# An order table for TensorE and VectorE in a fused attention and maxout kernel

## The chip, the cores and the metric

One core of one Trainium2 chip runs the whole kernel. The metric is the device time of one execution in microseconds (us); the median over several executions counts.

## The reference

Attention with queries pooled in pairs, then a feed-forward layer that takes the larger of two projections:

```python
# q, k, v: (8, 8, 1152, 64); w1, w2: (512, 1024); w_out: (1024, 512)
q_pool = q.reshape(B, H, S // 2, 2, D).mean(axis=3)
scores = (1.0 / np.sqrt(D)) * np.matmul(q_pool, k.transpose(0, 1, 3, 2))
attn = np.exp(scores - scores.max(-1)); attn = attn / attn.sum(-1)   # axes kept
x = np.matmul(attn, v)            # to (4608 tokens, 512), heads side by side
g = np.maximum(x @ w1, x @ w2)
out = g @ w_out                   # (4608, 512)
```

## The kernel before

**The work.** The 64 heads are taken two at a time: 32 pairs, four pairs to a batch. For each pair, GpSimd casts q, k and v to bf16 (`cast_q` adds the two pooled rows), k is transposed by a DMA (`ktrans`) or, for the first five pairs, on TensorE (`ktrans_pe`), and q by eight 32-partition transposes on VectorE (`qtrans_dve`, L378) or, for the first five pairs, on TensorE.

The scores of all pairs are one long row of columns, cut into 324 groups of 512 columns. One *score group* (`scores`, L516) is 2 to 8 matmuls; the two heads use rows 0 to 63 and 64 to 127 of the array. Its result fills one of the buffers `sps` (two PSUM banks), and ScalarE takes the exponential of it (L523) into the SBUF ring `et`. At first there are three such buffers. Once feed-forward work begins, at some 60 us, one of them is given to other work and the scores alternate between two (`ring`).

When all groups of a pair are through, its *weighted sums* come (`av_jobs`): one *rest block* with 64 columns of the array (18 matmuls, L437) and eight units of nine matmuls (L425), into two further banks. VectorE divides by the row sums (`norm`, L447 to L457) into `xnat`. A finished batch is transposed into `xT` by five DMAs (`xtrans`, L564); the first and the last batch are transposed on TensorE (`xtrans_pe`).

The feed-forward layer is computed as max(x w1, x w2) w_out = relu(x (w1 - w2)) w_out + x (w2 w_out). `h_pairs` (L728) makes the relu input and `p_pair` (L761) the output, in *units* of two matmuls of 64 rows each, which run beside each other on the two halves of the array; VectorE evacuates two banks at once (L737, L772). The second half of such a job swaps the two halves, and its first unit is a *fence*: it waits until TensorE's last write to these banks is complete. After the last score, the same work goes in single-bank jobs on all 128 rows (L701, L794), with ScalarE helping to evacuate. The weights are prepared in the first third (`w_cast`, `w_diff`, `w2t_job`, `w21_jobs`).

**Order.** Nothing is looped on the chip. The function plays through the work with a clock of its own: at each step it picks the next TensorE operation from the jobs in `lane`, by estimated readiness (`when`), rank and estimated cost (`op(..., cost=...)`). Its model has one cost per operation, a fixed signalling delay per engine (`LAT`), 0.1 us where TensorE's shape (`mode`) changes, and a single DMA pipe. What it emits stands in `plan.ops`, each operation with the operations it depends on (`deps`). `solve` then turns dependences into semaphore waits: it walks the list in order and leaves out every wait that an earlier wait of the engine already implies. `emit` writes each engine's operations in their order in the list, so an engine whose next operation isn't ready stops. Three orders hang together in this way: TensorE's 1471 operations, VectorE's 516, and those of ScalarE (370), GpSimd (105) and the DMA queue on SyncE (210).

The five modes of TensorE operations are "s" (two halves of 64 rows: scores and feed-forward pairs), "f" (all 128 rows: weighted sums, transposes and single-bank jobs), "c" (64 columns: rest blocks), and "z" (64 by 64: transposes of q). In the order before, neighbours differ in mode at 204 places.

Of the kernel before, what the change touches and what calls it, by code (L numbers as in the profile page):

```python
# [1 line left out]

# [9 lines left out]
COPY = mybir.ActivationFunctionType.Copy  # L12
ALU = mybir.AluOpType
AX = mybir.AxisListType


class Plan:
# [40 lines left out]
    def op(self, eng, fn, r=(), w=(), dma=None, cost=0.1, mode="f", after=(), solo=False,  # L58
           fence=False):
        n = len(self.ops)  # L60
        assert all(k in self.writer for k in r), r
        deps, raw = self.deps(r, w, after)
        prev = self.last.get(eng)
        if prev is not None and (solo or self.ops[prev]["solo"]):
            deps.add(prev)
            raw.add(prev)
        self.last[eng] = n
        t = self.when(eng, r, w, after, fence)
        if dma is not None:
            if not self.dma_free:  # L70
                t = 0.78
            self.free[eng] = t + (1.3 if mode == "t" else 0.5)
            a = max(self.free[eng] + 1.2, self.dma_free)
            self.dma_free = a + cost + (1.9 if a < 5.0 <= a + cost else 0.0)
            seen = self.dma_free + 0.7
        else:
            if eng == "PE" and mode != self.mode:
                t += 0.1
                self.mode = mode
            self.free[eng] = t + cost  # L80
            seen = t + cost + self.LAT[eng]
        self.ops.append(dict(eng=eng, fn=fn, deps=deps, raw=raw, dma=dma, w=tuple(w),
                             seen=seen, end=self.free[eng], solo=solo, fence=fence))
        for k in r:
            self.readers.setdefault(k, set()).add(n)
        for k in w:
            self.writer[k] = n
            self.readers[k] = set()
        return n

    def solve(self):
        ops = self.ops
        know = {}
        dma_seen = {}
        for n, o in enumerate(ops):
            eng = o["eng"]
            kn = know.setdefault(eng, {})
            o["waits"] = []
            for d in sorted(o["deps"], reverse=True):
                p = ops[d]  # L100
                if p["dma"] is None:
                    if p["eng"] == eng and not o["fence"] and (eng == "PE" or eng != "DVE" and d not in o["raw"]):
                        continue
                    key = p["eng"]
                else:
                    key = ("dma", p["dma"])
                if kn.get(key, -1) >= d:
                    continue
                o["waits"].append(d)
                for k, v in p["know"].items():  # L110
                    if kn.get(k, -1) < v:
                        kn[k] = v
                kn[key] = max(kn.get(key, -1), d)
            o["know"] = dict(kn)
            if o["dma"] is not None:
                dma_seen[o["dma"]] = dma_seen.get(o["dma"], 0) + 1
                o["count"] = 16 * dma_seen[o["dma"]]
        need = set()
        for o in ops:
            need.update(o["waits"])  # L120
        cnt = {}
        for n, o in enumerate(ops):
            if o["dma"] is None:
                o["inc"] = n in need
                if o["inc"]:
                    cnt[o["eng"]] = cnt.get(o["eng"], 0) + 1
                    o["count"] = cnt[o["eng"]]
        self.dma_total = {k: 16 * v for k, v in dma_seen.items()}
# [33 lines left out]
def bass_funnel_attn__then__act_maxout2_kernel(  # L162
# [32 lines left out]
    with ctx:  # L195
# [41 lines left out]
        plan = Plan()  # L237
# [8 lines left out]
        def setup():  # L246
            op("POOL", lambda g: g.memset(ident[:, :], 1.0), w=["id0"])
            op("POOL", lambda g: g.affine_select(
                ident[:, :], ident[:, :], pattern=[[1, P]], compare_op=ALU.is_equal,
                fill=0.0, base=0, channel_multiplier=-1), r=["id0"], w=["ident"])  # L250

            def ones(g):
                for s in range(3):
                    last = g.memset(vE[s][:, :, :, 64:66], 1.0)
                return last

            op("POOL", ones, w=["vE0", "vE1", "vE2"])
# [76 lines left out]
        def dve(fn, r, w, cost):  # L334
            op("DVE", fn, r=r, w=w, cost=cost)
# [267 lines left out]
        def w_cast(part, ct):  # L603
            if part == 0:
                dve(lambda e: e.tensor_reduce(
                    w2b[:, ct, :], w2f[:, ct, :].unsqueeze(2), AX.X, ALU.max),
                    [f"w2f{ct}"], [f"w2b{ct}"], 1.13)
            else:
                dve(lambda e: e.tensor_reduce(
                    wo[:, 2 * ct:2 * ct + 2, :], wof[:, 2 * ct:2 * ct + 2, :].unsqueeze(3), AX.X, ALU.max),  # L610
                    [f"wof{ct}"], [f"wo{2 * ct}", f"wo{2 * ct + 1}"], 1.13)
# [240 lines left out]
        line = []  # L852
# [5 lines left out]
        todo = []  # L858
# [135 lines left out]
        def burst_size():  # L994

            if turn_at[0] < NGR:
                return 1
            done = [b for b in range(B) if all(av_half.get(b * NHP + j) == 2 for j in range(NHP))]
            return 3 if done else 2
# [188 lines left out]
        while p_end[0] < NTOK:  # L1188
# [48 lines left out]
            else:  # L1237
# [3 lines left out]
                size = burst_size()  # L1241
# [10 lines left out]
        plan.free["PE"] = 1e9  # L1252
        flush()

        plan.solve()
        engines, dmas = plan.sems()
        sem = {n: ctx.enter_context(nc.semaphore("sem_" + n)) for n in engines + dmas}
# [49 lines left out]
```

## Time and profile before

| | |
|---|---|
| median of 7 runs | 378.08 us (377.7 to 380.06) |
| the profiled execution | 378.93 us, of which 377.2 us span |
| TensorE matmul busy | 360.3 us (96%) |
| ScalarE busy | 315.0 us (84%) |
| VectorE busy | 238.0 us (63%) |
| GpSimd busy | 124.9 us (33%) |
| granted TensorE clock | 1.0 throughout |
| last score group starts | 326.4 us |

The span is from the first to the last instruction of the profiled execution. Busy time of TensorE is modelled at the end of each matmul, and a matmul that stands waiting for its weights counts in part as busy; its starts are measured.

### The profile page before, as it was taken

The page shows a single profiled execution, that of the slowest core. Times are in us where ns is not written, and L with a number is a line of the kernel's source. Part 1 is how long each engine was busy: PE and PEld are TensorE (multiplying, and loading weights), DVE is VectorE, ACT ScalarE, POOL GpSimd, SP SyncE. Part 2 cuts the span into 40 slices and gives each one's busy share as a digit, 9 for nine tenths or more (in the row PEclk, how much of TensorE's full clock was granted, in tenths as well). Part 3 has the DMA queues.
Part 4 walks back from the last instruction along what each step waited for, and adds up shares of the span by engine and source line. Part 5 has one row for each costly group of instructions (what it writes and reads, how often), then busy time and mean ns, then how long its engine had stood idle before and what let it go on. Part 6 is the DMA issues. An engine that isn't in the chain of part 4 may idle for free.

```text
span 377.2 us, 12699 instructions
## 1 busy us (share of the span) xinstructions
PE 360.3 (96%) x5621; PEld 203.1 (54%) x5621; DVE 238.0 (63%) x516; ACT 315.0 (84%) x360; POOL 124.9 (33%) x111
## 2 busy tenths in 40 slices
PE   4899999999999999999999999998999999999996
PEld 2465556555555464555555555554655554665463
DVE  2685499866677667765686668765786635342231
ACT  4999799999999999999999999999899999811131
POOL 1359955562234233333333333332233010000000
PEclk9999999999999999999999999999999999999999
DMA  7999999999999799978898979997994431012324
GB/s 291 406 396 400 398 234 321 326 323 328 126 313 324 225 211 235 312 225 232 209 339 236 258 159 339 291 235 85 257 282 112 97 80 34 2 29 59 82 57 111
DMA packets 76823, 84.68 MB, mean 224 GB/s; under 512 B 49376, under 2 KB 49632, under 8 KB 76768
## 3 DMA queue, kind: packets, MB, share of 16 engines
q1 hardware_dynamic: 75888, 82.56, 79.3%
q10 hardware_dynamic: 880, 1.31, 0.9%
q8 instruction: 44, 0.72, 0.9%
q14 instruction: 11, 0.09, 0.1%
HBM read 62.91 MB, written 9.44 MB: 192 GB/s over the span
## 4 chain that ended last, share of the span: by engine, by line
PE 68%; ACT 19%; DVE 9%; issue 2%; DMA 1%; SPq 0%; DVEq 0%
ACT et L523 19%; PE sps L516 15%; PE sps L425 9%; PE sps L761 8%; PE fb L425 7%; PE sps L794 6%; DVE qpT L378 5%; PE fb L761 5%; PE fb L728 4%; PE sps L728 4%; PE sps L701 2%; PE fb L701 2%; PE sps L437 2%; PE fb L794 1%; PE fb L437 1%
## 5 line engine op out<-in xcount | busy, mean ns | idle before, releaser
L523 ACT ACTIVATE et<-sps 128x1024 bf16<-128x1024 f32 (+1 forms) x336 | 304.0, 1033 | 18.4 <-PE sps L516 17.0
L516 PE MATMUL sps<-qpT,kT 64*128 64x256 bf16 (+7 forms) x1162 | 120.4, 290 | 5.1 <-ACT et L523 1.7
L378 DVE STREAM_TRANSPOSE qpT<-qp 32x288 bf16<-32x288 bf16 x216 | 101.4, 469 | 34.1 <-PE sps L516 25.2
L324 POOL TENSOR_SCALAR vE<-vraw 128x1152 bf16<-128x1152 f32 x32 | 36.9, 1153 | 150.0 <-PE sps L425 89.9
L516 PEld LDWEIGHTS sps<-qpT,kT 64*128 64x128 bf16 x1162 | 39.8, 94 | 81.2 <-ACT et L523 64.6
L318 POOL TENSOR_TENSOR qp<-qraw 128x576 bf16<-128x576 f32 x30 | 42.1, 1404 | 12.3 <-DMA qraw<-in_q_dram 6.6
L425 PE MATMUL fb<-vE,et 128*128 128x65 bf16 x1152 | 40.7, 193 | 0.1
L425 PE MATMUL sps<-vE,et 128*128 128x65 bf16 x1152 | 40.4, 193 | 0.0
L425 PEld LDWEIGHTS fb<-vE,et 128*128 128x128 bf16 x1152 | 36.7, 97 | 4.9 <-issue 3.7
L285 POOL TENSOR_SCALAR kbf<-kraw 128x1152 bf16<-128x1152 f32 x31 | 35.7, 1151 | 10.3 <-DMA kraw<-in_k_dram 7.9
L425 PEld LDWEIGHTS sps<-vE,et 128*128 128x128 bf16 x1152 | 36.5, 97 | 4.1 <-issue 3.5
L728 PE MATMUL fb<-xT,wd 64*128 64x512 bf16 (+1 forms) x240 | 35.9, 373 | 1.6 <-issue 1.3
L728 PE MATMUL sps<-xT,wd 64*128 64x512 bf16 x224 | 33.0, 376 | 0.0
L761 PE MATMUL sps<-wo,stage 64*128 64x512 bf16 x224 | 31.9, 376 | 0.0
L761 PE MATMUL fb<-wo,stage 64*128 64x512 bf16 x192 | 27.6, 376 | 0.0
L737 DVE TENSOR_SCALAR stage<-fb 128x1024 bf16<-128x1024 f32 (+1 forms) x15 | 18.1, 1204 | 12.3 <-PE fb L728 12.2
L737 DVE TENSOR_SCALAR stage<-sps 128x1024 bf16<-128x1024 f32 x14 | 17.1, 1220 | 12.3 <-PE sps L728 11.9
L728 PEld LDWEIGHTS fb<-xT,wd 64*128 64x128 bf16 x240 | 11.2, 94 | 11.9 <-PE fb L728 2.1
L761 PE MATMUL sps<-w,xT 64*128 64x512 bf16 x112 | 16.6, 378 | 0.8 <-DVE xnat L457 0.6
L772 DVE COPY stage<-sps 128x1024 f32<-128x1024 f32 x7 | 8.6, 1223 | 12.2 <-PE sps L761 12.2
L794 PE MATMUL sps<-wo,stage 128*128 128x512 bf16 (+2 forms) x72 | 15.8, 355 | 0.0
L761 PEld LDWEIGHTS sps<-wo,stage 64*128 64x128 bf16 x224 | 10.7, 94 | 8.3 <-issue 0.4
(68 smaller groups left out, 278.3 us busy)
## 6 DMA issues: line engine op xcount, KB each, us to landing
kraw<-in_k_dram SPq DMA_DIRECT2D x32, 576.0 KB, 7.1
vraw<-in_v_dram SPq DMA_DIRECT2D x32, 576.0 KB, 7.8
qraw<-in_q_dram SPq DMA_DIRECT2D x31, 576.0 KB, 6.2
out_dram<-stage SPq DMA_DIRECT2D x19, 256.0 KB, 4.8
out_dram<-stage SPq DMA_DIRECT2D x23, 128.0 KB, 2.4
xT<-in_moe_w_dram SPq DMA_DIRECT2D x4, 512.0 KB, 10.1
stage<-in_moe_w_out_dram SPq DMA_DIRECT2D x4, 512.0 KB, 13.6
stage<-in_moe_w_dram SPq DMA_DIRECT2D x4, 512.0 KB, 13.6
```

The source lines that it names most:

```text
L285: op("POOL", lambda g: g.tensor_scalar(kbf[s][:, :, :, :].rearrange("p t h d -> p h t d"), kraw[r][:, :, :, :], 1.0, 1.0, ALU.mult, ALU.mu ...
L318: op("POOL", lambda g: g.tensor_tensor(qpf[s][:, :, :], qraw[r][:, :, 0, :], qraw[r][:, :, 1, :], ALU.add), r=[f"qraw{r}"], w=[f"qp{s}.0", ...
L324: op("POOL", lambda g: g.tensor_scalar(vE[r][:, :, :, 0:D].rearrange("p t h d -> p h t d"), vraw[r][:, :, :, :], 1.0, 1.0, ALU.mult, ALU.m ...
L378: op("DVE", lambda e: e.transpose(view[dst:dst + 32, :, 32 * pb:32 * pb + 32], qpf[s][src:src + 32, :, 32 * db:32 * db + 32]), r=[f"qp{s}. ...
L425: last = e.matmul(fb[m][:, sb * 66:sb * 66 + 65], et[:, a:a + P], vE[vs][:, t, half, 0:65], start=(t == 0), stop=(t == NT - 1))
L516: last = e.matmul(sps[r][:, h, col:col + hi - lo], kT[i % 3][rows(h), t, :], qpT[i % 3][rows(h), lo:hi], start=True, stop=True)
L523: op("ACT", lambda e: e.activation(et2[:, :, c:c + z - a], sps[r][:, :, a - g * W:z - g * W], EXP, scale=scale), r=[f"s{r}"], w=keys + ([f ...
L701: return e.matmul(fb[m][:, 0:size], wd[:, ct, ft * P:(ft + 1) * P], xT[:, ct, n0:n1], start=(ct == 0), stop=(ct == NC_ - 1))
L728: last = e.matmul(fb[m + k][:, 0:size], wd[z, ct, (f0 + k) * P:(f0 + k + 1) * P], xT[z, ct, n0:n1], start=(turn == 0 and ct == 0), stop=(t ...
L737: dve(lambda e: e.tensor_scalar_max(gT[:, f0:f0 + 2, g0:g0 + size], wide[m // 2][:, :, 0:size], 0.0), [f"f{m}", f"f{m + 1}"], w + [f"f{m}" ...
L761: last = e.matmul(fb[m + k][:, :], lhs, rhs, start=(turn == 0 and j == 0), stop=(turn == 1 and j == NC_ + NF - 1))
L794: return e.matmul(fb[m][:, 0:c1 - c0], lhs, rhs[:, c0:c1], start=(j == 0), stop=(j == NC_ + NF - 1))
```

## The change

Two strings are added, one for TensorE and one for VectorE. Each character (with a "~" ahead of it for a distance over 39) says which of the operations that are left, in the order in which the planner emitted them, comes next: "0" the first, "1" the second, and so on. `arrange` takes the planner's list, deals it out by engine, puts the two engines in the order of the strings, and merges the engines' lists again so that each operation stands behind those that it depends on. `solve` then works on the new list. The dependences are those of the order before; the operations themselves, and the order on ScalarE, GpSimd and the DMA queue, are as they were.

```diff
+ORDER = {
+    "PE": (
+        "0000100100020000101000100002003003010021030001000000000201000101100002:0088:09080062220051333533"
...
+    ),
+    "DVE": (
+        "0000000010101000000020010200000000000000010000044857000200122210?0603354544492119265250304134727"
...
+    ),
+}
...
+    def arrange(self, order):
+        line = {}
+        for n, o in enumerate(self.ops):
+            line.setdefault(o["eng"], []).append(n)
+        for eng, picks in order.items():
+            rest = line[eng]
+            line[eng] = [rest.pop(40 * (len(c) - 1) + ord(c[-1]) - 48) for c in re.findall("~*[0-X]", picks)]
+            assert not rest
+        at = {key: 0 for key in line}
+        new = {}
+        ops = []
+        while len(ops) < len(self.ops):
+            size = len(ops)
+            for key, todo in line.items():
+                while at[key] < len(todo) and all(d in new for d in self.ops[todo[at[key]]]["deps"]):
+                    n = todo[at[key]]
+                    at[key] += 1
+                    new[n] = len(ops)
+                    ops.append(self.ops[n])
+            assert len(ops) > size
+        for o in ops:
+            o["deps"] = {new[d] for d in o["deps"]}
+            o["raw"] = {new[d] for d in o["raw"]}
+        self.ops = ops
...
         plan.free["PE"] = 1e9
         flush()
 
+        plan.arrange(ORDER)
         plan.solve()
```

A stretch of TensorE's order before, and about the same stretch after, with S for a score group, h and p for feed-forward units (L728, L761), r for a rest block, a for a weighted-sum unit, and a count where one repeats:

```
before  S r a3 S S a5 S h S h4 S h3 S h3 S h3 S h2 S h3 S r a3 S S a5 S h S p3 S
after   S h2 r S h2 S a4 S S a4 S h3 S h3 S h3 S h3 S h3 S h2 S h3 S h r S a4 S S a4 S h3 S p3 S
```

More of the change, by code (lines that the diff above doesn't have):

```diff
@@ L1 @@
+import re
 from contextlib import ExitStack
@@ L14 @@
 AX = mybir.AxisListType
+ORDER = {
+    "PE": (
+        "0000100100020000101000100002003003010021030001000000000201000101100002:0088:09080062220051333533"
+        "330022004060220100344353340000400005500000001001101107445440024005000511611005006002041000300400"
+        "030004;05026330220040050005000050030005611100500004060000500004000030060003003055000060700006000"
+        "600060006004474450007115007:000:000904:0020900080000800004:9044404830000600700006007222071004:;;"
+        "9::;;908400247011060006000600060000700500;90030590100060070000600777<788787777070000060070400600"
+        "603305200041114104000500300014500005000400003053022420104;<<4;;90:80060004360006007777;887888870"
+        "7000805580448400800006007000777<9086666800744900090004888070005007600799997844445000604063026000"
+        "60005006000702522226722226000600060006000600085:555:75555500070007605700373307010600005007305222"
+        "26722220600061116010600060000500700500080335:0000080:0000900080000700080062692557:52229000900090"
+        "0090009000:05899959:8555:000:006:600:030:0119100080009047444489444490009001911108119110080000900"
+        "005090030059000070007000060060000500702223842225226007111160006000600085:55859755550007000700474"
+        "44700006000040666668666666600040555044504034335000040000300003<304000033000002000200300202100000"
+        "001000010000000000000000010000000004002803355152412210000000000000000000000000000000000000000000"
+        "000000000000000000000000000000000000000000000000000000000000000000000000000000000000000000000000"
+        "000000000000000000000000000000000000000000000000000000000000000000000000000000000000000000000000"
+        "0000000000000000000000000000000"
+    ),
+    "DVE": (
+        "0000000010101000000020010200000000000000010000044857000200122210?0603354544492119265250304134727"
+        "120130277343331538;8777035094853=022331222208818240454486361160005995655340220=550845212=3016472"
+        "0042664334:09;8278714048102577541033333331603577065504453>>:0999421057:244072020421331121;;<0676"
+        "60150455975132444413302:;0;999083>8;23:02988877003033626240022233248;7415;;78772104230==919880?1"
+        "61224920773065534436>44100343333303;;;;2::0082034:8:;:;;2920025<<8<;<<;6231105443122211110000010"
+        "000010000000000000000000000000000000"
+    ),
+}
 class Plan:
```

## The prediction

> **What bounds the kernel now.** I read the page's head first, for which engine is full; then busy time by stage, the totals of waits, and one repeating stretch of the timeline. The first fence is the page (busy time with its share of the span, then 40 slices in tenths).
>
> ```profile
> span 377.2 us, 12699 instructions
> PE 360.3 (96%) x5621; PEld 203.1 (54%) x5621; DVE 238.0 (63%) x516; ACT 315.0 (84%) x360; POOL 124.9 (33%) x111
> ...
> PE   4899999999999999999999999998999999999996
> ...
> ACT  4999799999999999999999999999899999811131
> ```
>
> TensorE is full to the end, ScalarE until 326 us, where the last softmax exponential is done. What follows, 51 us of feed-forward work, has TensorE alone. The view by stage (stretch, length, then busy us of PE, PEld, DVE, ACT, POOL):
>
> ```profile
> 60.00:326.00 266.00, 261.11 (x4372) 144.63 (x4370) 185.39 (x402) 251.91 (x279) 90.19 (x74) 1.00 0.87 226
> ```
>
> So the 266 us in the middle carry 252 us of ScalarE. TensorE's 261 is too flattering, since a matmul counts as busy while its weights wait; its slack has to be found in starts. Waits (engine, tile, line, releaser: us, times, longest):
>
> ```profile
> PEld sps L516 <- ACT et L523: 64.6, 180, 1.0
> ...
> ACT et L523 <- PE sps L516: 17.0, 39, 2.5
> ```
>
> The two engines wait for each other: scores (L516) need a free score buffer, which the exponential (L523) gives back, and the exponential needs scores. The 64.6 us are mostly covered by the matmul in front; the 17.0 us are bare. The timeline shows one turn of the pattern (start, us, engine, line, count, idle before):
>
> ```profile
> 108.86 0.39 PE L516 MATMUL sps<-qpT,kT 64*128 64x320 bf16 x4
> 109.18 0.47 PE L437 MATMUL sps<-vE,et 128*64 128x65 bf16 x18
> 109.59 0.99 PE L425 MATMUL sps<-vE,et 128*128 128x65 bf16 x27
> 110.51 0.61 PE L516 MATMUL sps<-qpT,kT 64*128 64x384 bf16 x8
> 111.06 1.53 PE L425 MATMUL sps<-vE,et 128*128 128x65 bf16 x45
> 112.52 0.39 PE L516 MATMUL sps<-qpT,kT 64*128 64x512 bf16 x2
> 112.75 0.38 PE L728 MATMUL fb<-xT,wd 64*128 64x512 bf16 x2
> 112.96 0.38 PE L516 MATMUL sps<-qpT,kT 64*128 64x512 bf16 x2
> 113.18 0.81 PE L728 MATMUL fb<-xT,wd 64*128 64x512 bf16 x6
> 113.83 0.38 PE L728 MATMUL sps<-xT,wd 64*128 64x512 bf16 x2
> 114.04 0.38 PE L516 MATMUL sps<-qpT,kT 64*128 64x64 bf16 x4
> 114.26 0.81 PE L728 MATMUL sps<-xT,wd 64*128 64x512 bf16 x6
> 114.94 0.39 PE L516 MATMUL sps<-qpT,kT 64*128 64x128 bf16 x4
> ```
> ```profile
> 110.94 7.61 ACT L523 ACTIVATE et<-sps 128x1024 bf16<-128x1024 f32 x8 [0.30 <-PE sps L516]
> ```
>
> Prices from starts. A score group S is 0.22 us (114.04 to 114.26). A feed-forward unit (two matmuls) is 0.216 (113.18 to 113.83 is three). A weighted-sum unit (nine matmuls, L425) is 0.272: 111.06 to 112.52 is five, and 0.10 over. That 0.10 comes at each change of the array's shape: S to a weighted sum takes 0.314 over the trace where S to a feed-forward unit takes 0.218, and the last weighted-sum unit before an S takes 0.367 where one before its like takes 0.272. So **a switch costs 0.095**. In steady state a score comes each 0.917 us: ScalarE's pace.
>
> Taking for each kind of neighbours its usual unhindered distance from each actual distance leaves 24.3 us of TensorE stall: 7.6 before 60 us, 16.1 from 60 to 320, 0.6 later. The ending stretch isn't stalled. In the middle, some 80 scores after a feed-forward unit start 0.04 late and 17 start 0.25 late; there are single losses of 0.47 (three times), 0.69, and this one, where a feed-forward unit came before its input (no engine is named; its source is an xT transpose by DMA):
>
> ```profile
> 263.67 0.82 PE L728 MATMUL fb<-xT,wd 64*128 64x512 bf16 x6 [1.32 <-issue]
> ```
>
> **What the skill says.** The Trainium skill, page "TensorEngine Tiling (Array Packing)", section Key Properties: changing the tiling mode drains TensorE. The trace agrees: 0.095 us at each change between 64-row, 128-row and 64-column matmuls, nothing between two users of one shape. Page "TensorE: Matmul & The Clock Gate", Part 3, The mechanism: a weight load is pulled ahead of running matmuls where it doesn't conflict. That agrees with the scores that waited being 0.04 late at the least: their weights couldn't be ahead. Page "Perfetto Trace Analysis", section Tensor Engine Instruction: a matmul's end is an estimate; hence starts alone are used here.
>
> **The change, part by part.** Read against the kernel's own list, the TensorE table moves 1099 of 1471 operations, by 12 places earlier to 22 later; the VectorE table 437 of 516, by 15 earlier to 24 later. Nothing is added or removed, and ScalarE, GpSimd and the DMA queue keep their order. The last score stays at the same place with the same work ahead of it, and TensorE's list behind its 1206th entry is unchanged. So the end moves as the last score moves; ScalarE and VectorE in the tail only follow.
>
> *Added: switches.* 204 become 240: 36 x 0.095 = **+3.4 us**, 31 of them after 60 us (2.9). Fifteen are column-tiled rest blocks (L437) straight before scores, a pair the trace lacks. Nearest row: rest block to weighted sum, the same sort of switch, 0.407 with the block. Bounds: 0 to 0.2 each, so 0 to 3 us; I take 0.095.
>
> *Removed: stall.* Name a gap by the units between two scores: c the rest block, a4 four weighted sums, 3 three feed-forward units. Before, a turn is mostly "3 3 3 2 3 ca3 0 a5 1 4". With the prices a 3 is 0.218 + 3 x 0.216 = 0.866, under ScalarE's 0.917, so TensorE waits 0.05 each time and 0.27 at the 2; ca3 is 0.321 + 0.407 + 2 x 0.272 + 0.367 = 1.64, which two buffers don't cover: the exponential starts 0.30 us after its engine went idle, some 0.4 off its pace (the ACT line above). TensorE's sum is 9.27 us for ten scores; the 0.46 that it waits and the 0.57 that ScalarE starves (0.4 at ca3, 0.17 at a5) make 9.73.
>
> After, threes drop from 109 to 76 and fours rise from 18 to 44, and the weighted sums are cut oftener: "3 3 3 3 3 1c a4 0 a4" is typical. Sum: 5 x 0.866 + 0.913 + 1.497 + 0.228 + 1.497 = 8.47 for nine, against 9 x 0.917 = 8.25 for ScalarE. Followed by hand from a state in which scores just wait: 1c meets its buffer on time, the first a4 starves ScalarE by 0.26, the 0 waits 0.11, the second a4 starves nobody, and the next threes run 0.01 to 0.27 behind their buffers, so none waits. Stall is 0.11 at most against 0.46, at the price of one or two switches.
>
> Limit of the gain: TensorE needs 266 - 16.4 (stall, 60 to 326) + 2.9 = 252.5 us in the middle, ScalarE its 251.9. Two engines this level, with two buffers between, don't both run full. Of 16.4 us I leave 7: 27 turns at 0.11 (3.0), about 60 scores that still find their weights late (2.4), half of the single losses (1.6). The saving is 16.4 - 7 - 2.9 = **6.5 us**. Before 60 us I take zero: there ScalarE is busy without a break from 20 to 40 us and the loads move 400 GB/s, so half a microsecond of switches stands against as much regained.
>
> *Moved on VectorE.* Evacuations and normalisations go 2 to 5 places earlier, the transposes of q (L378, 0.469 us each) 5 later on the mean. Queued behind a transpose is at worst an evacuation of 1.22 us that frees two banks. I cost this at nothing: VectorE is 63% busy, and a transposed q is wanted most of a turn later. In the new list the nearest reuse of a bank comes 1.41 us of TensorE work after its last writer, as against 0.88 before; the work from the last weighted sum of a batch to the first unit on its transposed rows grows in four places by 0.5 to 2.8 us (by 1.0 where 1.3 was lost) and shrinks in three by 0.23 at most. If that cover is gone, each late evacuation stops TensorE for up to 0.5 us, as three did. Stores issue as evacuations end, so on the SP queue they don't come later.
>
> Sum: the profiled run took 378.93 us (span 377.2), 0.85 above the median of 378.08. 378.93 - 6.5 = 372.4, or on the median's footing **371.6**. Bounds: all stall but the start's gone, 365; switches at their dear end and a stall of 9 left, 375.
>
> **Rivals.** (1) ScalarE becomes the bound: exponentials pause at each fresh split, and TensorE's waits come back as score waits. For it: 252 against 252.5. Half the intended saving is left, about 375. (2) The gain is hidden: VectorE or DMA lateness gives it back at transposed inputs, as at 263 us; 378. Against it: those distances grow. (3) **Slower**: the switches aren't repaid. Place: the cut weighted sums; price: 3.4 us at 0.095, up to 5 with dear rest blocks. It decides once less than 3.4 of the stall goes, so if scores still wait 0.04 and 0.25 as often as before: 382. Against it: the hand-followed turn. (4) The table does nothing: excluded in its letter, as most places move.
>
> **How the numbers follow.** 0.3% (1.1 us) is about what a measurement of this kernel can tell from no change. Forecast (367 to 375) 0.68; rival 1, 0.12; rival 2, 0.06; rival 3, 0.14. Faster 0.80, same 0.06, slower 0.14. The range goes from 366 to 378.6: it leaves out the slow case and a little below.
>
> **What would show it.** Right: the wait of L523 for L516 falls from 17.0 to under 10 us; the last score starts at 320 instead of 326.4; the 1.32 at the block after 260 us shrinks; matmul counts and the last 51 us stay. Wrong: L523's wait unchanged with more L425-to-L516 switches (rival 3), or new VectorE releasers in front of L728 and L761 (rival 2).

## The result and the profile after

The changed kernel takes **380.87 us** in the median (378.36 to 383.75, 24 runs), the kernel before 377.92 (377.4 to 380.86, 61 runs): a recorded ratio of **1.0063**, 95% interval 1.0047 to 1.0079 (it is not the quotient of the medians, which is 1.0078; the later ratios are taken in the same way). It is slower, by less than one per cent, where the prediction said 371.6 and faster. The profiled execution took 382.42 us, 380.3 of it span. It is one of five executions of the change, of 382.4 to 383.8 us, that were granted 0.996 of the clock; the others, of 378.4 to 381.9 us, were granted 0.998 or more.

The head of the changed kernel's page: busy time, then the slices of TensorE, ScalarE and of TensorE's clock.

```profile
span 380.3 us, 12682 instructions
## 1 busy us (share of the span) xinstructions
PE 359.4 (95%) x5621; PEld 212.1 (56%) x5621; DVE 237.0 (62%) x516; ACT 316.4 (83%) x360; POOL 124.5 (33%) x111
...
PE   3799989999999999999978999999999999999996
...
ACT  4999899999999999999968999999989999811131
...
PEclk9999999999999999999989999999999999999999
```

The work is the same. TensorE and ScalarE have a dent at 190 to 209 us, the 21st and 22nd slice, and the clock one in the 21st. By stage, ScalarE did less in the middle 266 us than before (249.7 us against 251.9):

```profile
60.00:326.00 266.00, 258.77 (x4338) 152.01 (x4339) 184.05 (x401) 249.72 (x276) 88.52 (x73) 0.99 0.84 226
```

The waits (line numbers are 56 higher than before: scores L572, exponential L579, normalisation L503 to L513, q transposes L434, feed-forward units L784 and L817):

```profile
PEld sps L572 <- ACT et L579: 24.5, 84, 1.5
ACT et L579 <- PE sps L572: 18.4, 39, 2.5
...
PEld sps L817 <- DVE xnat L513: 4.4, 6, 1.5
...
PEld fb L784 <- DVE xnat L513: 2.8, 5, 0.9
```

TensorE's wait for the exponential fell from 64.6 to 24.5 us, as intended. What is new is feed-forward units that wait for a normalisation. Before, the same two rows had 1.2 us, shown here, and 0.7 us:

```profile
PEld sps L761 <- DVE xnat L457: 1.2, 2, 0.6
```

ScalarE still lacks scores for 18.4 us, so the 40 us bought nothing on its side.

TensorE's stall from 60 to 328 us, by what ended it, in this and all later profiles. It is worked out as in the prediction: start-to-start time less the usual one for the pair of operations, put to the last of the operations waited for. "None" is stall for which none of these ended less than 0.25 us before; parts under 0.5 us in sum are left out, and the parts of a row miss its total by up to 0.7 us. The kernel before comes to 14.1 us here, where the prediction counted 16.1 for 60 to 320 us; only differences between rows are used.

| us | score buffer | normalisation | evacuation, q transposes | DMA | fence | none | all |
|---|---|---|---|---|---|---|---|
| before | 9.5 | 1.6 | 0.6 | 1.5 | 0.9 | 0.0 | 14.1 |
| the change | 2.7 | 5.7 | 1.3 | 0 | 0.8 | 3.7 | 13.7 |
| e1, transposes back | 2.7 | 2.5 | 4.7 | 0 | 0.7 | 4.1 | 14.2 |
| e2, VectorE's table alone | 4.4 | 22.2 | 8.2 | 0 | 1.3 | 6.5 | 43.3 |
| e3, short transposes, change | 3.4 | 1.0 | 0 | 0 | 0.2 | 0.5 | 4.9 |
| e4, short transposes, planner | 10.8 | 0.6 | 0.4 | 0 | 1.6 | 0.1 | 13.6 |
| e5, VectorE relisted | 3.4 | 0.6 | 0 | 0 | 0.4 | 1.3 | 5.3 |
| e8, planner, VectorE relisted | 10.0 | 0.6 | 0.4 | 0.5 | 1.2 | 0.2 | 13.0 |
| e6, light loads, change | 2.9 | 5.5 | 1.3 | 0 | 0.2 | 0.1 | 9.8 |
| e7, light loads, planner | 9.8 | 1.6 | 0.5 | 0 | 0.9 | 0.0 | 12.8 |

The span closes on it: no change of stall before 60 us (11.8 in both), -0.4 in the middle, +3.4 for the 36 switches, which makes 3.0 of the 3.1 us.

So of the score waits 6.8 us went, and the lost DMA wait of 1.5. They came back as 4.1 of normalisations, 0.7 of evacuations and transposes, and 3.7 for which no operation answers. Here is a late normalisation, in the timeline of VectorE and of TensorE (changed kernel):

```profile
270.86 1.22 DVE L793 TENSOR_SCALAR stage<-fb 128x1024 bf16<-128x1024 f32 x1 [2.37 <-PE fb L784]
272.38 1.23 DVE L828 COPY stage<-sps 128x1024 f32<-128x1024 f32 x1 [0.29 <-PE sps L817]
273.63 3.72 DVE L434 STREAM_TRANSPOSE qpT<-qp 32x288 bf16<-32x288 bf16 x8
277.39 0.19 DVE L503 RECIPROCAL rc<-sps 128x5 f32<-128x5 f32 x1
277.62 0.45 DVE L508 TENSOR_TENSOR xnat<-sps,rc 64x64 bf16<-64x64 f32 x2
278.10 0.42 DVE L513 TENSOR_TENSOR xnat<-sps,rc 128x256 bf16<-128x256 f32 x1
278.44 0.17 DVE L503 RECIPROCAL rc<-sps 128x4 f32<-128x4 f32 x1
278.65 0.42 DVE L513 TENSOR_TENSOR xnat<-sps,rc 128x256 bf16<-128x256 f32 x1
```
```profile
276.15 1.26 PE L481 MATMUL sps<-vE,et 128*128 128x65 bf16 x36
277.35 0.39 PE L572 MATMUL sps<-qpT,kT 64*128 64x64 bf16 x4
277.58 0.81 PE L784 MATMUL fb<-xT,wd 64*128 64x512 bf16 x6
278.22 0.38 PE L572 MATMUL sps<-qpT,kT 64*128 64x128 bf16 x4
279.13 1.04 PE L784 MATMUL sps<-xT,wd 64*128 64x512 bf16 x8 [0.52 <-DVE xnat L513]
```

VectorE first stands idle for 2.37 us with an evacuation at its head, whose bank TensorE hasn't written yet. Four of the eight transposes behind it had had their inputs since 259 us. When it may go on, all eight run in a row until 277.35. The bank of the pair's first half has its last sum in the first of the four units that start at 276.15 and is complete at some 276.6, so its normalisation starts 0.8 us late; the second half's bank is complete at 277.4. The two normalisations stand in one block of 1.7 us that ends at 279.07, and TensorE's next unit, which needs these banks, starts 0.69 us late.

The 3.7 us without a releaser are one event, TensorE's timeline at 191 us and the stretches around it (length, busy times, then the clock, DMA share and GB/s):

```profile
190.97 0.81 PE L784 MATMUL fb<-xT,wd 64*128 64x512 bf16 x5
193.73 0.58 PE L784 MATMUL fb<-xT,wd 64*128 64x512 bf16 x1 [1.96 <-issue]
193.74 1.00 PE L572 MATMUL sps<-qpT,kT 64*128 64x512 bf16 x2
```
```profile
194.00:197.00 3.00, 3.00 (x18) 1.64 (x16) 0.00 (x0) 1.54 (x2) 0.41 (x1) 0.50 1.02 387
197.00:200.00 3.00, 3.00 (x38) 1.97 (x36) 1.77 (x3) 2.76 (x4) 0.00 (x0) 0.98 0.96 359
```

One of two matmuls of a unit runs, and its twin starts 2.3 us later (2.1 of it stall), with no semaphore between; then TensorE runs at half clock for 3.4 us (0.50 in the first stretch). The page names a small queue:

```profile
q8 instruction: 44, 0.72, 0.8%
```

I read its 44 pieces of 16 KB as TensorE's own instructions, 256 each: 44 x 256 is 11,264, TensorE has 11,242 matmuls and weight loads, and a piece comes for about every 256 of them. In the trace a piece usually starts to arrive when TensorE is 200 to 400 instructions past the last but one boundary, if the count has a boundary at each 256. Piece 22 of the changed kernel (counted from 0) starts at 191.5 us, at 449. It has landed at 192.4, and TensorE doesn't advance until 193.7. Before, the same piece started at 233 instructions, and the latest of all at 393.

### The profile page after: what moved, and what is told of

Same layout as the page of the kernel before. It is cut to its first block, busy times and chain, and to the rows that moved or that the text cites. A ratio compares the mean times of both kernels' runs of the same rounds, so it can differ in the third digit from the quotient of the medians.

```text
span 380.3 us, 12682 instructions
## 1 busy us (share of the span) xinstructions
PE 359.4 (95%) x5621; PEld 212.1 (56%) x5621; DVE 237.0 (62%) x516; ACT 316.4 (83%) x360; POOL 124.5 (33%) x111
## 4 chain that ended last, share of the span: by engine, by line
PE 67%; DVE 11%; ACT 9%; issue 7%; DMA 3%; POOL 2%; SPq 0%; POOLq 0%; DVEq 0%
PE sps L572 15%; ACT et L579 9%; PE sps L817 8%; PE sps L481 7%; PE fb L481 7%; PE fb L817 6%; PE sps L784 6%; PE sps L850 5%; DVE qpT L434 5%; PE fb L784 4%; DMA qraw<-in_q_dram 2%; PE sps L757 2%; DVE xnat L513 2%; PE fb L757 2%; PE fb L695 1%
## 5 line engine op out<-in xcount | busy, mean ns | idle before, releaser
L579 ACT ACTIVATE et<-sps 128x1024 bf16<-128x1024 f32 (+1 forms) x336 | 305.4, 1015 | 19.9 <-PE sps L572 18.4
L572 PE MATMUL sps<-qpT,kT 64*128 64x256 bf16 (+7 forms) x1162 | 122.3, 290 | 3.8 <-ACT et L579 1.9
L434 DVE STREAM_TRANSPOSE qpT<-qp 32x288 bf16<-32x288 bf16 x216 | 100.1, 467 | 9.7 <-POOL qp L374 2.5
L572 PEld LDWEIGHTS sps<-qpT,kT 64*128 64x128 bf16 x1162 | 46.4, 95 | 60.4 <-ACT et L579 24.5
L481 PE MATMUL sps<-vE,et 128*128 128x65 bf16 x1152 | 41.7, 193 | 0.0
L784 PE MATMUL fb<-xT,wd 64*128 64x512 bf16 (+1 forms) x240 | 38.0, 380 | 2.7 <-issue 2.0
L784 PE MATMUL sps<-xT,wd 64*128 64x512 bf16 x224 | 35.8, 383 | 1.2 <-DVE xnat L513 0.7
L817 PE MATMUL sps<-wo,stage 64*128 64x512 bf16 x224 | 31.7, 376 | 0.0
L817 PE MATMUL fb<-wo,stage 64*128 64x512 bf16 x192 | 28.1, 376 | 0.0
L793 DVE TENSOR_SCALAR stage<-fb 128x1024 bf16<-128x1024 f32 (+1 forms) x15 | 18.0, 1202 | 13.6 <-PE fb L784 13.3
L503 DVE RECIPROCAL rc<-fb 128x5 f32<-128x5 f32 (+1 forms) x32 | 5.9, 185 | 25.8 <-PE fb L481 25.5
L503 DVE RECIPROCAL rc<-sps 128x4 f32<-128x4 f32 (+1 forms) x32 | 5.9, 183 | 23.0 <-PE sps L481 22.7
L817 PE MATMUL sps<-w,xT 64*128 64x512 bf16 x112 | 17.1, 378 | 2.3 <-DVE xnat L513 2.0
L784 PEld LDWEIGHTS fb<-xT,wd 64*128 64x128 bf16 x240 | 11.3, 95 | 10.7 <-DVE xnat L513 2.8
L784 PEld LDWEIGHTS sps<-xT,wd 64*128 64x128 bf16 x224 | 10.3, 95 | 12.0 <-PE sps L784 2.2
## 6 DMA issues: line engine op xcount, KB each, us to landing
stage<-in_moe_w_dram SPq DMA_DIRECT2D x4, 512.0 KB, 14.2
```

The source lines that it names most:

```text
L434: op("DVE", lambda e: e.transpose(view[dst:dst + 32, :, 32 * pb:32 * pb + 32], qpf[s][src:src + 32, :, 32 * db:32 * db + 32]), r=[f"qp{s}. ...
L481: last = e.matmul(fb[m][:, sb * 66:sb * 66 + 65], et[:, a:a + P], vE[vs][:, t, half, 0:65], start=(t == 0), stop=(t == NT - 1))
L572: last = e.matmul(sps[r][:, h, col:col + hi - lo], kT[i % 3][rows(h), t, :], qpT[i % 3][rows(h), lo:hi], start=True, stop=True)
L579: op("ACT", lambda e: e.activation(et2[:, :, c:c + z - a], sps[r][:, :, a - g * W:z - g * W], EXP, scale=scale), r=[f"s{r}"], w=keys + ([f ...
L784: last = e.matmul(fb[m + k][:, 0:size], wd[z, ct, (f0 + k) * P:(f0 + k + 1) * P], xT[z, ct, n0:n1], start=(turn == 0 and ct == 0), stop=(t ...
L793: dve(lambda e: e.tensor_scalar_max(gT[:, f0:f0 + 2, g0:g0 + size], wide[m // 2][:, :, 0:size], 0.0), [f"f{m}", f"f{m + 1}"], w + [f"f{m}" ...
```

## The experiments

**Theory A**: the new TensorE order does save the score waits, and VectorE's order gives them back, because its fixed places put q transposes ahead of normalisations. **Theory B**: the new TensorE order isn't better; late normalisations are a symptom. **Theory C**, for the rest: TensorE's instructions came late among the transfers.

### e1: q transposes back in their old places

```diff
 VectorE's list: (t a transpose, r/x/n a normalisation, E an evacuation)
-the change's list
+its other 300 operations in the change's order; each t again behind as many of them as in the planner's list
```

> TensorE's table as in the change; in VectorE's table only the 216 q transposes (L434 in the changed kernel) are put back to their old places among the other VectorE operations (on the mean 4.7 places earlier), the rest keeps the new order. Theory A (the gain was real and was given back by normalisations that stand behind q transposes): TensorE's waits for normalisations, 5.7 us after 60 us in the changed kernel, fall to about 2, its waits for score buffers stay near 2.7 (9.5 before); the time is 373 to 376. Theory B (the new TensorE order is no better, and the late normalisations are a symptom): score-buffer waits come back as the others go, the time is 378 or more.

Measured: 381.06 us (379.87 to 384.02), ratio 1.0077 (1.0048 to 1.0106). Neither theory's picture came. Normalisation waits fell to 2.5 and score waits stayed at 2.7, as A has it, but 4.0 us of evacuation waits appeared. VectorE and TensorE of this run:

```profile
150.51 1.23 DVE L793 TENSOR_SCALAR stage<-fb 128x1024 bf16<-128x1024 f32 x1 [1.91 <-PE fb L784]
151.65 1.90 DVE L434 STREAM_TRANSPOSE qpT<-qp 32x288 bf16<-32x288 bf16 x4
153.56 1.22 DVE L793 TENSOR_SCALAR stage<-sps 128x1024 bf16<-128x1024 f32 x1
```
```profile
154.84 0.47 PE L493 MATMUL sps<-vE,et 128*64 128x65 bf16 x18 [1.24 <-DVE stage L793]
```

The old places don't suit the new TensorE order: four transposes now stand ahead of an evacuation, and the rest block that needs its bank stops for 1.24 us. The stall without a releaser came at the same operation (2.5 us at 197.9). The time is in B's range and not in A's, but the score waits that B asks for didn't come back. The wait moved; the run doesn't decide between A and B.

### e2: VectorE's table without TensorE's

```diff
 ORDER = {
-    "PE": (...),
     "DVE": (...),
```

> VectorE's table alone, TensorE in the planner's order. Theory A: score waits as before (about 9.5 us), no added switches (204), but normalisations late behind transposes as in the changed kernel, some 2 to 4 us more of them: 380 to 383. Theory B: VectorE's order is no cost of its own: 377.5 to 379.

Measured: 419.23 us (415.92 to 421.27), ratio 1.1065 (1.102 to 1.111), far outside both. TensorE waits 22 us for normalisations. One of them, in TensorE's timeline of this run:

```profile
79.79 0.61 PE L766 MATMUL fb<-xT,wd 64*128 64x512 bf16 x2 [3.33 <-DVE xnat L495]
```

The bank had its last sum at 75.2 us. VectorE worked all the time between, on transposes and on the other half's normalisation, which its list puts ahead. The half clock, for 3.4 to 6.8 us, shows up five times: once at 20 us, and four times behind idle stretches of TensorE of 2.2 to 3.5 us. What the run teaches isn't the price of VectorE's table in the changed kernel, where the two tables fit far better, but how steep the price of a misfit is.

### e3 and e4: short q transposes

```diff
-                view[dst:dst + 32, :, 32 * pb:32 * pb + 32],
-                qpf[s][src:src + 32, :, 32 * db:32 * db + 32]),
+                view[dst:dst + 32, 0:4, 32 * pb:32 * pb + 32],
+                qpf[s][src:src + 32, 0:4, 32 * db:32 * db + 32]),
```

> The changed kernel with both tables, but each q transpose by VectorE moves 4 of its 9 column blocks, so its result is not the reference's; the count and the order of operations and all waits stay. VectorE gets some 45 to 55 us less work. Theory A: the waits for normalisations fall from 5.7 to under 2 us and the time to 374 to 376, well under its control with the planner's order. Theory B: no nearer than before, within 1 us of the control or above it.

> The control of the last one: the planner's order (a table of its own places, so that the merging of the list is in it), q transposes of 4 of 9 blocks. Theory A: 1 to 2 us less than before at the most (normalisations cost TensorE 1.6 us there): 376 to 378. Theory B: the same, and the changed order with short transposes is not below it.

The two kernels leave out five of nine blocks of each q transpose. Measured: 373.92 us with the change's order (372.79 to 375.79; ratio to before 0.9886, 0.9857 to 0.9914), 377.95 with the planner's (377.2 to 380.6; 0.9996, 0.9982 to 1.0011). VectorE's busy time fell by 35 us (237.0 to 202.4; 45 to 55 were expected). The short transposes do nothing for the planner's order and 7 us for the change's: normalisation waits go from 5.7 to 1.0, score waits rise only to 3.4, and piece 22 of the instructions came in time, which is part of the 7 us. That is A against B: the TensorE order is 4 us better than the planner's once VectorE is out of its way. Its last score starts at 320.4 us, where the prediction had 320.

The trace of e4 also holds the instruction stall, in the planner's order. TensorE stops inside one weighted-sum unit at 21.9 us, at 449 instructions past the last but one boundary, while piece 0 arrives (21.4 to 22.4), and 3.4 us at half clock follow from 23.9:

```profile
23.98 0.46 PE L481 MATMUL fb<-vE,et 128*128 128x65 bf16 x5 [1.86 <-issue]
```

A second, shorter stop of this kind at 194.5 us, inside a score group and at 445 instructions, is about 0.6 of the 1.6 us that the table puts to the fence.

### e5 and e8: VectorE listed anew

```diff
 VectorE's list, a stretch of it:
-n t r t x r t t x n n t t t E t t t E E ...
+n n t8 r x x r n n E t3 E E ...
```

TensorE's table stays. For e5, VectorE's operations behind the first q transpose are sorted along the TensorE times of e3: what empties a bank goes first once the bank is written; transposes fill the rest, unless a bank falls due within 0.3 us. For e8 the same rule is used along the times of the kernel before, with the planner's TensorE order.

> TensorE's table as in the change, full q transposes, and a new order for VectorE alone: behind the first q transpose its operations are listed anew along the TensorE times of the run with short transposes, an evacuation or a normalisation ahead of any transpose once its bank is written, a transpose where none of these falls due within 0.3 us. Theory A (the gain of the TensorE order is real, and where VectorE's transposes stand decides whether it is kept): waits for normalisations and evacuations together, 6.4 us after 60 us in the changed kernel and 7.2 with the transposes put back, fall below 2.5; score waits stay near 3; 373 to 376. Theory B (VectorE hasn't the room, whatever the order): 378 to 381, with the same waits in other places.

> The control of the relisted run: TensorE in the planner's order, VectorE listed anew by the same rule along the times of the kernel before. Theory A: normalisations and evacuations cost TensorE 2.2 us after 60 us before, so at most 1 to 2 us come off, and the score waits of 9.5 us stay: 376.5 to 378.5. If the relisting alone made the gain, it would be at 375 too.

Measured: e5 **373.12 us** (371.52 to 373.97), ratio 0.9871 (0.985 to 0.9892); e8 377.76 (377.11 to 380.22), ratio 1.0 (0.9985 to 1.0016). e5 does the full work in the change's TensorE order, and takes 7.7 us less than with the change's VectorE table. Not all of it is waits for VectorE: at piece 22 TensorE stands idle for 0.8 us instead of 2.0, and no half clock follows. e5 beats both kernels, and e8 says that the sorting by itself gains nothing. Here are the head of the page and the waits of e5:

```profile
span 370.4 us, 12692 instructions
## 1 busy us (share of the span) xinstructions
PE 355.5 (96%) x5614; PEld 210.2 (57%) x5621; DVE 239.0 (65%) x516; ACT 314.2 (85%) x360; POOL 125.0 (34%) x111
```
```profile
PEld sps L572 <- ACT et L579: 33.3, 111, 1.5
...
ACT et L579 <- PE sps L572: 11.2, 28, 1.2
...
PEld sps L817 <- DVE xnat L513: 0.5, 1, 0.5
```

VectorE is as busy as ever; only its order differs. Feed-forward units hardly wait for normalisations (0.5 us in the row that had 4.4), and now ScalarE's bare wait for scores is down too, from 17.0 before to 11.2. The same place as in the changed kernel's timeline above:

```profile
263.52 1.23 DVE L828 COPY stage<-sps 128x1024 f32<-128x1024 f32 x1 [0.29 <-PE sps L817]
264.77 2.88 DVE L434 STREAM_TRANSPOSE qpT<-qp 32x288 bf16<-32x288 bf16 x6
267.78 0.20 DVE L503 RECIPROCAL rc<-sps 128x5 f32<-128x5 f32 x1
...
269.05 0.42 DVE L513 TENSOR_TENSOR xnat<-sps,rc 128x256 bf16<-128x256 f32 x1
```
```profile
269.37 0.38 PE L572 MATMUL sps<-qpT,kT 64*128 64x128 bf16 x4
269.59 1.03 PE L784 MATMUL sps<-xT,wd 64*128 64x512 bf16 x8
```

Six transposes instead of eight stand ahead. They end at 267.65, before the first half's bank is complete, so its normalisation starts at once. The last normalisation ends at 269.47, and the unit that started 0.91 us after the scores ahead of it (0.69 of it stall) starts 0.22 us after them, at 269.59. The last score starts at 319.6 us.

### e6 and e7: light loads

```diff
-                kraw[s][...], k[...]),
+                kraw[s][...][:, :, 0:(NT if i < 6 else 2) * D], k[...][:, :, 0:(NT if i < 6 else 2) * D]),
 (v likewise; q with 2 of its 9 rows from pair 6 on)
```

> The changed kernel with the loads of q, k and v from pair 6 on cut to 2 of 9 blocks (the rest is left over from an earlier pair, so the result is not the reference's); all waits and compute stay. Theory C (the 2.1 us in which TensorE waited for nothing at 191 us, and the half clock after it, were its next 16 KB of instructions, late among transfers): its fetch there comes with under 420 instructions past the boundary, no such stall after 60 us, no half clock, and the times scatter less; the waits for normalisations stay near 5, so 377.5 to 379. Rival: the stall is there without the loads too (transposing transfers or TensorE itself).

> The control: the planner's order with the same light loads. Theory C: within 1 us of before, 377 to 378, with less scatter. If loads cost the planner's order more than that (a rival, in which late loads and not instructions are the price), 375 or less.

Measured: 379.32 us with the change's order (377.99 to 380.58; ratio 1.0012, 0.9998 to 1.0027), 378.18 with the planner's (377.4 to 380.75; 1.0011, 0.9997 to 1.0025). In the middle the core moves 100 GB/s instead of 226 (e6, by stage):

```profile
60.00:326.00 266.00, 260.84 (x4403) 152.83 (x4402) 186.63 (x408) 253.30 (x280) 88.44 (x73) 1.00 0.48 100
```

Piece 22 starts at 253 instructions instead of 449, the stall without releaser is 0.1 us instead of 3.7, no half clock comes with it, none of the executions was granted less than 0.998 of the clock, and the range of times is 2.6 us instead of 5.4. Normalisation waits stay at 5.5. The median is 0.3 us over what was expected. The loads cost the planner's order nothing, but its range didn't shrink as expected: 3.4 us, against 3.2 of the kernel before. In the profiled run the loads' price in the change is that of the late piece, 3.7 us; in the median the loads cost some 1.5 us (380.87 - 379.32). That this too is late instructions is likely but not shown, since the change was profiled in one execution only. The run also parts the two causes: with the stall gone, the change is still 1.1 us behind its control (379.32 - 378.18), and the waits that it has more of are those for VectorE. Which of the transfers holds the piece up wasn't tried.

## Why the prediction was wrong

**What bounds the kernel, and what the order saves: right.** The score waits were forecast to fall by a hand-followed turn; they fell from 9.5 to 2.7 us and stay at 3.4 where the order gets its due (e3, e5). The 1.49 us at the feed-forward block behind the DMA transposes is gone.

**Switches: right.** 36 at 0.095 make 3.4; the starts of the changed kernel show the same price. The pair that the trace lacked, a rest block straight before scores, takes 0.406 us with the block, as against 0.407 in front of a weighted sum; the dear end of the bound wasn't needed. Two details were off, without weight in the sum: of the fifteen rest blocks twelve stand straight before scores and three before other 64-row work, and the "1c" of the typical turn, 0.913 in the forecast, is 0.93 by these starts (0.218 + 0.309 + 0.406).

**"Moved on VectorE ... I cost this at nothing": this step failed.** It cost 4.1 us of normalisations and 0.7 of evacuations and transposes. It rested on the mean shift (evacuations 2 to 5 places earlier), on VectorE's 63%, and on TensorE work between a bank's last writer and its next user. None of them sees a queue: what counts is what VectorE still has ahead of a bank's normalisation when the bank is written, out of runs of up to eight transposes of 0.47 us, 3.7 us in all. The text put "at worst an evacuation" behind a transpose and didn't ask what a bank waits for behind eight of them. The price it named if the cover was gone, 0.5 us a time, was too small as well (1.35 at the longest).

**Not in the sum at all: TensorE's instructions.** A piece that was late among the loads, 2.1 us, and the half clock behind it made 3.7 us in the profiled run and, if e6 is read so, 1.5 in the median. The trace of before shows a piece that started 393 instructions past the boundary, near the end at 449; the prediction didn't read that queue.

**The sum.** Of the 6.5 us that were forecast, the score waits and the single DMA wait gave 8.3 and the switches took 3.4 (3.0 in the middle): 4.9 remain. VectorE took 4.8 and the instructions 3.7, which leaves 3.6 on the wrong side; the span has 3.1. e5 shows the forecast mechanism without the failed step, and with less of the instruction stall: 373.12, inside the forecast's own 367 to 375.

**The rivals.** Number 3 named the right sign and the wrong mechanism: score waits did not stay. Number 2, VectorE's lateness at the inputs, named the right engine, but at transposed inputs and with a price that only hides the gain. The signs given for the right case failed where they should: ScalarE's bare wait stayed at 18.4 (under 10 was forecast, and even e5 has 11.2), and the last score started at 329.5 instead of 320. The sign for rival 2, new VectorE releasers ahead of the feed-forward units, is what the profile has.

## What to carry to other kernels

Two orders that were made for each other have to be checked as queues: for each bank, count the work that the emptying engine has in front of its operation when the bank is written, and what that engine would be waiting for. Put work that is due late (here the transposes) behind anything that frees a buffer, and let it fill gaps; a fixed place that suits one order of the other engine is a stall in another. A small share of busy time says nothing about such a queue.

## What the runs showed of the hardware

In these traces TensorE's instructions come by DMA in pieces that fit 16 KB for 256 instructions, and a piece can be late among other transfers. All five stops at such a piece (the change at 191.4 us, e1 at 195.2, e4 at 21.9 and 193.8, e5 at 188.0) came 445 to 449 instructions past the last but one boundary and left TensorE idle for 0.5 to 2.3 us; each ended 1.2 to 1.5 us after the piece had landed, and no semaphore shows it ("issue" in the profile).

The half clock came in stretches of 3.4 us or twice that. It followed idle stretches of TensorE of 1.96 us (the change), 2.29 (e1), 1.86 (e4) and 2.2 to 3.5 (e2), but not one of 2.08 us in e2 at 171.8 us, nor the 1.2 us of the longest wait for a normalisation in the change. So these runs give no length from which it comes. In the changed kernel the half clock cost another 1.6 us. The price of a change of array shape was 0.09 to 0.10 us for every pair of kinds that can be compared.
